# Feed-forward token tiles of 512, 512, 512 and 256 instead of four of 448, on one core

## The chip, the core and the metric

The program runs on one core of one Trainium2 chip. The metric is the device time of one execution in microseconds (us), the median of several runs. A core has a matrix engine (PE in the profile, with PEld for its weight loads), a vector engine (DVE), a scalar engine (ACT), a POOL engine that does next to nothing here, and SP, which issues the DMA transfers.

## What is computed

Three stages in a row: sigmoid attention over 4 batches x 12 heads x 448 tokens, then a feed-forward block with a maximum over three projections, then one with a slope for negative values. In short:

```
scores = scale * q @ k.T - log(S)                # 4 x 12 heads, S = 448, head_dim 64
x = sigmoid(scores) @ v                          # -> 1792 tokens x 768
h = max(max(x @ w1, x @ w2), x @ w3)             # 768 -> 768
y = h @ w_out                                    # 768 -> 768
p = y @ w_in                                     # 768 -> 2048
g = max(p, 0) + alpha * min(p, 0)
out = g @ w_out2                                 # 2048 -> 768
```

The weights come as 64-bit floats, viewed as pairs of 32-bit words; everything else is 32-bit.

## The kernel before

All activations lie with features on the 128 partitions and tokens along the free axis. For accuracy every feed-forward operand is split into a high and a low part, both of type float32r, and a product is made of three matmuls: weight-low x token-high, weight-high x token-low, weight-high x token-high. Weight loads and matmuls come in pairs: each matmul has a weight load of its own.

**Attention.** 24 pairs (batch b, pair of heads p). For each pair: 24 matmuls into `sc` (four chunks of keys, three products, two heads in the two halves of the rows), four sigmoids on ACT (L278), and 16 float32 matmuls of the pair before into `pav` (L287). ACT then copies `pav` into the high part `xh` (L297) and DVE subtracts to get the low part `xl` (L298).

**Feed-forward.** Tokens are cut into four tiles of 448, one for each batch. One accumulation in PSUM is a group: for a tile t and 128 output features, all inner blocks times three products. Stages are named by their PSUM tile: `b` (three projections, 18 weight units, 18 matmuls to a group), `c` (output of the first block, 6 units, 18 matmuls), then eight rounds of `d` (two units, 18 matmuls to a group) and `e` (6 groups for each t, each 6 matmuls over the two blocks of that round). All these matmuls are issued in `group` (L356). PSUM has 8 buffers for them (`ps_m`). DVE and ACT take the sums out: a copy or maximum for `b`, a split for `c`, the slope function for `d`, and for `e` an addition into `acc` (L488; in the first round a copy).

The work around the matmuls is in a hand-written order. `pending` holds the steps that turn a raw weight unit into its high and low part (8 per half unit, 6 of them on DVE); after each group of `b` and `c` 6 of them are issued (`run_pending(6)`), in `d` 8 and in `e` 2 per group (`weave`). In the last `e` round each finished `acc` is transposed on DVE one group later (`finish`, L420), and `store` (L504) sends it out in four transfers: a whole tile at a time, the last tile in two cuts.

Of the kernel before, what the change touches and what calls it, by code (L numbers as in the profile page):

```python
# [19 lines left out]
def kernel(  # L20
# [25 lines left out]

    nc = tc.nc

    B, H, S, D = q.shape
# [11 lines left out]
    HF = UN // 2  # L63
    scale = 1.0 / math.sqrt(D)
    neg_log_s = -math.log(S)

# [17 lines left out]
    SK = 2  # L84
# [108 lines left out]
            ops += [first, shift, sign, hi, power, rest, diff, lo]  # L193
        return ops

    def tmp(nm):
        return tpool.tile([P, S], F32, tag="tmp", name=nm, bufs=5)

    def xy_tile(nm, t):
        return (  # L200
            xpool.tile([P, KDM, S], F32R, tag=f"xyh{t}", name=f"{nm}h{t}"),
            xpool.tile([P, KDM, S], F32R, tag=f"xyl{t}", name=f"{nm}l{t}"),
        )


    def attention(apool, ps_s, ps_v):
# [73 lines left out]
        def av_pair(i):  # L280
            b, p = pairs[i]
            vt = prepped.pop(i)[-1]
            pav = ps_v.tile([P, 512], F32, tag="pv", name=f"pav{i}")
            for c in range(NCH):
                a = at.pop((i, c))
                for j in range(2):
                    nc.tensor.matmul(  # L287
                        pav[j * D : (j + 1) * D, :S],
                        vt[:, j * NCH + c, :],
                        a[:, j, :],  # L290
                        start=(c == 0),
                        stop=(c == NCH - 1),
                    )
            if p == 0:
                xt[b] = xy_tile("x", b)
            xh, xl = xt[b]
            nc.scalar.copy(xh[:, p, :], pav[:, :S])  # L297
            nc.vector.tensor_sub(xl[:, p, :], pav[:, :S], xh[:, p, :].bitcast(F32))  # L298

        n = len(pairs)  # L300
        load_pair(0)
# [31 lines left out]
    xt, yt, ht = {}, {}, {}  # L333


    def terms(n, wu, col, src):

        hi, lo = wu

        def cross(r):  # L340
            xh, xl = src(r)
            return [(lo[:, col(r)], xh), (hi[:, col(r)], xl)]

        def main(r):
            return [(hi[:, col(r)], src(r)[0])]

        got = []
        for r in range(n - 1):
            got += cross(r)
        for r in range(n - 1):  # L350
            got += main(r)
        return got + cross(n - 1) + main(n - 1)

    def group(ps, mms):
        for z, (lt, rh) in enumerate(mms):
            nc.tensor.matmul(ps, lt, rh, start=(z == 0), stop=(z == len(mms) - 1))  # L356

    def rowcol(r):
        return slice(r * P, (r + 1) * P)
# [4 lines left out]
        for _ in range(min(n, len(pending))):  # L364
            pending.pop(0)()

    def hl(pool, tag, nm):
        return (
            pool.tile([P, S], F32R, tag=f"{tag}h", name=f"{nm}h"),
            pool.tile([P, S], F32R, tag=f"{tag}l", name=f"{nm}l"),  # L370
        )

    def split(dst, src):
        hi, lo = dst
        nc.scalar.copy(hi, src)
        nc.vector.tensor_sub(lo, src, hi.bitcast(F32))

    def ff1(hpool, ps_m):
        u = 0
        for m in range(KF1):  # L380
            cur = {}
            for j in range(3):
                if u:
                    pending.extend(conv_ops(u + 1))
                for t in range(B):
                    ps = ps_m.tile([P, 512], F32, tag="mm", name=f"b{m}_{j}_{t}")[:, :S]
                    group(ps, terms(KDM, wsp[u], rowcol, lambda r: (xt[t][0][:, r, :], xt[t][1][:, r, :])))
                    run_pending(6)
                    if j == 0:
                        cur[t] = tmp(f"mx{m}_{t}")  # L390
                        nc.scalar.copy(cur[t], ps)
                    else:
                        nc.vector.tensor_tensor(out=cur[t], in0=ps, in1=cur[t], op=ALU.max)  # L393
                    if j == 2:
                        ht[m, t] = hl(hpool, f"h{m}_{t}", f"h{m}_{t}")
                        split(ht[m, t], cur[t])
                run_pending(99)
                wsp.pop(u)
                u += 1
        for m in range(KDM):  # L400
            pending.extend(conv_ops(u + 1))
            for t in range(B):
                ps = ps_m.tile([P, 512], F32, tag="mm", name=f"c{m}_{t}")[:, :S]
# [4 lines left out]
                yh, yl = yt[t]  # L408
                split((yh[:, m, :], yl[:, m, :]), ps)
            run_pending(99)  # L410
            wsp.pop(u)
            u += 1
        return u

    def ff2(gpool, ps_m, u):
# [2 lines left out]

        def finish(t, m, a, o):
            nc.vector.transpose(out=o[:, :, m, :], in_=a.rearrange("p (n i) -> p n i", i=32))  # L420
            cuts = [KDM] if t < B - 1 else [2, KDM]
            if m + 1 in cuts:
                store(t, ([0] + cuts)[cuts.index(m + 1)], m + 1, o)

        late, turn = [], []

        def prelu(m, t, ps, g):
            r_, n_ = tmp(f"r{m}_{t}"), tmp(f"n{m}_{t}")

            def parts():  # L430
                nc.scalar.activation(r_, ps, AF.Relu)
                nc.scalar.activation(n_, ps, AF.Relu, scale=-1.0)  # L432
# [12 lines left out]

            return [parts, join, hi, lo]
# [9 lines left out]
        for s in range(NS):  # L456
            pending.extend(conv_ops(u + SK))
            pending.extend(conv_ops(u + SK + 1))
            for f in range(SK):
                for t in range(B):  # L460
                    ps = ps_m.tile([P, 512], F32, tag="mm", name=f"d{s}_{f}_{t}")[:, :S]
                    group(ps, terms(KDM, wsp[u], rowcol, lambda r: (yt[t][0][:, r, :], yt[t][1][:, r, :])))
                    gt[f, t] = hl(gpool, f"g{f}_{t}", f"g{SK * s + f}_{t}")
# [7 lines left out]
            for t in range(B):  # L471
                if last:
                    ot[t] = xpool.tile([P, NB32, KDM, 32], F32, tag=f"xyh{t}", name=f"o{t}")
                for m in range(KDM):
                    ps = ps_m.tile([P, 512], F32, tag="mm", name=f"e{s}_{m}_{t}")[:, :S]
                    mms = []
                    for f in range(SK):
                        hi, lo = (x[:, m * P : (m + 1) * P] for x in wsp[u + f])
                        gh, gl = gt[f, t]
                        mms += [(lo, gh), (hi, gl), (hi, gh)]  # L480
                    group(ps, mms)
                    weave(late, 2)
                    late = []
                    if s == 0:
                        acc[m, t] = gpool.tile([P, S], F32, tag=f"acc{m}_{t}", name=f"acc{m}_{t}")
                        nc.scalar.copy(acc[m, t], ps)
# [12 lines left out]


    def store(t, m0, m1, o):
        for g in range(4):
            c0 = g * (DM // 4)
            nc.sync.dma_start(  # L504
                out=out[t * S : (t + 1) * S, c0 + 32 * m0 : c0 + 32 * m1].rearrange(
                    "(n i) f -> i n f", i=32
                ),
                in_=o[32 * g : 32 * g + 32, :, m0:m1, :].rearrange("i n m j -> i n (m j)"),
            )
# [53 lines left out]
```

## Time and profile before

| | |
|---|---|
| time, median of 3 runs | 984.21 us (983.95 to 984.31) |
| the profiled execution: time / span of its instructions | 984.14 us / 982.4 us |
| PE busy / DVE busy / ACT busy | 98% / 65% / 37% of the span |
| matmuls, and weight loads | 4992 of each |
| of these in the feed-forward stages (`b`, `c`, `d`, `e`) | 4032 |
| bytes read / written | 60.56 MB / 5.51 MB |

The span runs from the first to the last instruction; 1.7 us of the execution lie around it. A busy time is the union of the instructions of an engine; matmuls overlap one another, so the time that one adds is read from the distance between two starts and not from its own duration.

### The profile page before, as it was taken

The page shows a single profiled execution, that of the slowest core. Times are in us where ns is not written, and L with a number is a line of the kernel's source. Part 1 is how long each engine was busy: PE and PEld are TensorE (multiplying, and loading weights), DVE is VectorE, ACT ScalarE, POOL GpSimd, SP SyncE. Part 2 cuts the span into 40 slices and gives each one's busy share as a digit, 9 for nine tenths or more (in the row PEclk, how much of TensorE's full clock was granted, in tenths as well). Part 3 has the DMA queues.
Part 4 walks back from the last instruction along what each step waited for, and adds up shares of the span by engine and source line. Part 5 has one row for each costly group of instructions (what it writes and reads, how often), then busy time and mean ns, then how long its engine had stood idle before and what let it go on. Part 6 is the DMA issues. An engine that isn't in the chain of part 4 may idle for free.

```text
span 982.4 us, 12885 instructions
## 1 busy us (share of the span) xinstructions
PE 962.8 (98%) x4992; PEld 831.7 (85%) x4992; DVE 639.4 (65%) x1257; ACT 360.2 (37%) x635; POOL 0.2 (0%) x4
## 2 busy tenths in 40 slices
PE   6999999999999999999999999999999999999995
PEld 3455557999999999999999999999999999999994
DVE  5667771655464565565578368868587785869765
ACT  5677772122221222122236552332414334152410
POOL 0000000000000000000000000000000000000000
PEclk9999999999999999999999999999999999999998
DMA  7777750211221112112122122212122121212017
GB/s 128 134 148 139 136 106 1 65 49 49 65 65 47 51 49 63 51 51 62 50 67 76 51 65 64 65 33 57 41 65 65 49 66 33 65 49 65 17 39 186
DMA packets 158990, 66.92 MB, mean 68 GB/s; under 512 B 116944, under 2 KB 154832, under 8 KB 158928
## 3 DMA queue, kind: packets, MB, share of 16 engines
q1 hardware_dynamic: 158928, 66.09, 27.4%
q8 instruction: 39, 0.64, 0.3%
q14 instruction: 23, 0.19, 0.1%
HBM read 60.56 MB, written 5.51 MB: 67 GB/s over the span
## 4 chain that ended last, share of the span: by engine, by line
PE 98%; SPq 1%; DVE 0%; DMA 0%; issue 0%; DVEq 0%
PE b L356 27%; PE e L356 24%; PE d L356 24%; PE c L356 9%; PE pav L287 8%; PE sc L271 7%; SPq L222 1%; DMA kr<-in_k_dram 0%; DVE kt L243 0%; DVE qt L243 0%; DVE acc L488 0%; DVE o L420 0%; DVEq L559 0%; SPq L229 0%; DVE qh L250 0%
## 5 line engine op out<-in xcount | busy, mean ns | idle before, releaser
L174 ACT CAST wh<-wt 128x384 fp32r<-128x384 f32 x112 | 57.6, 514 | 290.8 <-DVE wt L161 290.8
L356 PE MATMUL b<-xh,wl 128*128 128x448 f32 x432 | 158.0, 366 | 0.0
L356 PE MATMUL b<-xl,wh 128*128 128x448 f32 x432 | 158.0, 366 | 0.0
L356 PE MATMUL d<-yl,wh 128*128 128x448 f32 x384 | 140.4, 366 | 0.0
L356 PE MATMUL d<-yh,wl 128*128 128x448 f32 x384 | 140.4, 366 | 0.0
L488 DVE TENSOR_TENSOR acc<-e,acc 128x448 f32<-128x448 f32 x168 | 102.8, 618 | 19.1 <-PE e L356 17.7
L356 PE MATMUL b<-xh,wh 128*128 128x448 f32 x432 | 111.0, 366 | 0.0
L356 PE MATMUL d<-yh,wh 128*128 128x448 f32 x384 | 98.7, 366 | 0.0
L278 ACT ACTIVATE a<-sc,bias_s 112x896 f32<-112x896 f32 x96 | 89.1, 1008 | 14.9 <-PE sc L271 14.5
L356 PEld LDWEIGHTS b<-xh,wl 128*128 128x128 f32 x432 | 81.2, 188 | 7.1 <-issue 0.7
L356 PEld LDWEIGHTS b<-xh,wh 128*128 128x128 f32 x432 | 81.2, 188 | 6.3
L356 PEld LDWEIGHTS b<-xl,wh 128*128 128x128 f32 x432 | 81.3, 188 | 6.2
L158 DVE TENSOR_SCALAR wt<-wt 128x384 uint32<-128x384 uint32 x112 | 39.6, 353 | 71.1 <-ACT wt L150 71.0
L287 PE MATMUL pav<-a,vt 112*64 112x448 f32 x384 | 77.2, 545 | 0.0
L435 DVE SCALAR_TENSOR_TENSOR r<-n,nalpha,r 128x448 f32<-128x448 f32 x64 | 43.7, 683 | 51.4 <-ACT n L432 51.4
L356 PEld LDWEIGHTS d<-yh,wh 128*128 128x128 f32 x384 | 72.2, 188 | 5.6
L356 PEld LDWEIGHTS d<-yl,wh 128*128 128x128 f32 x384 | 72.2, 188 | 5.6
L356 PEld LDWEIGHTS d<-yh,wl 128*128 128x128 f32 x384 | 72.2, 188 | 5.6
L191 DVE TENSOR_TENSOR wl<-wt,ws 128x384 fp32r<-128x384 f32 x112 | 62.5, 558 | 4.8 <-DVE wt L188 0.5
L177 DVE SCALAR_TENSOR_TENSOR ws<-wr,ws 128x384 f32<-128x384 uint32 x112 | 62.5, 558 | 3.8
L161 DVE SCALAR_TENSOR_TENSOR wt<-wr,wt 128x384 uint32<-128x384 uint32 x112 | 62.3, 556 | 3.0
L393 DVE TENSOR_TENSOR mx<-b,mx 128x448 f32<-128x448 f32 x48 | 29.9, 623 | 52.1 <-PE b L356 52.1
(97 smaller groups left out, 1566.4 us busy)
## 6 DMA issues: line engine op xcount, KB each, us to landing
wr<-in_moe_w_out_dram SPq DMA_DIRECT2D x44, 384.0 KB, 3.1
wr<-in_moe_w_dram SPq DMA_DIRECT2D x36, 384.0 KB, 3.2
wr<-in_moe_w_in_dram SPq DMA_DIRECT2D x32, 384.0 KB, 3.2
kr<-in_k_dram SPq DMA_DIRECT2D x96, 56.0 KB, 3.3
qr<-in_q_dram SPq DMA_DIRECT2D x96, 56.0 KB, 2.6
vt<-in_v_dram SPq DMA_DIRECT2D x24, 224.0 KB, 3.5
out_dram<-o SPq DMA_DIRECT2D x12, 336.0 KB, 5.4
out_dram<-o SPq DMA_DIRECT2D x4, 224.0 KB, 3.9
```

The source lines that it names most:

```text
L158: nc.vector.tensor_scalar(st["T"], st["T"], 3, None, ALU.logical_shift_left)
L161: nc.vector.scalar_tensor_tensor(out=st["T"], in0=st["r"][:, :, 1], scalar=0x80000000, in1=st["T"], op0=ALU.bitwise_and, op1=ALU.bitwise_or,)
L174: nc.scalar.copy(part(0), seen(st["T"]))
L177: nc.vector.scalar_tensor_tensor(out=st["R"].bitcast(F32), in0=st["r"][:, :, 0], scalar=2.0**-52, in1=st["R"].bitcast(F32), op0=ALU.mult, ...
L191: nc.vector.tensor_add(part(1), seen(st["T"]), seen(st["R"]))
L271: nc.tensor.matmul(sc[:KC, j, :S], kk[r, c * KC : (c + 1) * KC], qq[r], start=(z == 0), stop=(z == 2),)
L278: nc.scalar.activation(a, sc[:KC, :, :S], AF.Sigmoid, bias=bias_s[:KC], scale=scale)
L287: nc.tensor.matmul(pav[j * D : (j + 1) * D, :S], vt[:, j * NCH + c, :], a[:, j, :], start=(c == 0), stop=(c == NCH - 1),)
L356: nc.tensor.matmul(ps, lt, rh, start=(z == 0), stop=(z == len(mms) - 1))
L393: nc.vector.tensor_tensor(out=cur[t], in0=ps, in1=cur[t], op=ALU.max)
L435: nc.vector.scalar_tensor_tensor(out=r_, in0=n_, scalar=nalpha[:, m : m + 1], in1=r_, op0=ALU.mult, op1=ALU.add,)
L488: nc.vector.tensor_tensor(out=acc[m, t], in0=ps, in1=acc[m, t], op=ALU.add)
```

## The change

The 1792 tokens are cut without regard to the batches: three tiles of 512 and one of 256. In the last tile the high and the low part of the tokens lie side by side in one 512-wide tile, so that weight-high is multiplied with both in one matmul of 512 columns; weight-low takes the high part alone, 256 columns. The sum then stands in two halves of a PSUM tile, which `whole` adds up (an ACT copy of one half and a DVE addition) before it is used; in `e` both halves are added into `acc` one after the other. The attention copies a batch's columns into the one or two token tiles that they fall in.

```diff
+    T = B * S
+    TW = 512
+    spans = [(c, min(TW, T - c)) for c in range(0, T, TW)]
+    NT = len(spans)
+    HW = spans[-1][1]
...
+            parts = []
+            for t, (c0, w) in enumerate(spans):
+                c, e = max(c0, b * S), min(c0 + w, b * S + S)
+                if c < e:
...
+            for xh, _, ps in parts:
+                nc.scalar.copy(xh, ps)
+            for xh, xl, ps in parts:
+                nc.vector.tensor_sub(xl, ps, xh.bitcast(F32))
...
         def cross(r):
-            xh, xl = src(r)
+            xh, xl, both = src(r)
+            if both is not None:
+                return [(hi[:, col(r)], both), (lo[:, col(r)], xh)]
             return [(lo[:, col(r)], xh), (hi[:, col(r)], xl)]
...
+    def whole(ps, t, nm):
+
+        if t < NT - 1:
+            return ps
+        s = tmp(nm, t)
+        nc.scalar.copy(s, ps[:, HW:])
+        nc.vector.tensor_tensor(out=s, in0=ps[:, :HW], in1=s, op=ALU.add)
+        return s
...
-                    else:
-                        nc.vector.tensor_tensor(out=acc[m, t], in0=ps, in1=acc[m, t], op=ALU.add)
+                        nc.scalar.copy(acc[m, t], ps[:, TW - w :])
+                    for h in range(s == 0, TW // w):
+                        part = ps[:, TW - (h + 1) * w : TW - h * w]
+                        nc.vector.tensor_tensor(out=acc[m, t], in0=part, in1=acc[m, t], op=ALU.add)
```

On PE, in the last `e` round, the first group of the last token tile (`e_0_3`: feature block 0, tile 3; `g_3` are the tokens, `wh` and `wl` the weights) before the change:

```order
L356 MATMUL e_0_3_8671<-g_3h,wl_8250 128x448
L356 MATMUL e_0_3_8671<-g_3l,wh_8249 128x448
L356 MATMUL e_0_3_8671<-g_3h,wh_8249 128x448
L356 MATMUL e_0_3_8671<-g_3h,wl_8325 128x448
L356 MATMUL e_0_3_8671<-g_3l,wh_8324 128x448
L356 MATMUL e_0_3_8671<-g_3h,wh_8324 128x448
```

The same place now, with the last two matmuls of the 512-wide tile ahead of it:

```order
L382 MATMUL e_5_2_8499<-g_2l,wh_8170 128x512
L382 MATMUL e_5_2_8499<-g_2h,wh_8170 128x512
L382 MATMUL e_0_3_8509<-g_3_8202,wh_8095 128x512
L382 MATMUL e_0_3_8509<-g_3_8202,wl_8096 128x256
L382 MATMUL e_0_3_8509<-g_3_8320,wh_8170 128x512
L382 MATMUL e_0_3_8509<-g_3_8320,wl_8171 128x256
```

The group has four matmuls, of 512 and 256 columns in turn; the groups of the other three tiles keep their number and are 512 wide.

On DVE, in the same round, before: one addition into `acc` for each group, and behind it the transposition of the group before.

```order
L488 TENSOR_TENSOR acc_2_5052<-e_5_2_8661,acc_2_5052 128x448
L420 STREAM_TRANSPOSE o_8611<-acc_2_5043 128x14x32
L488 TENSOR_TENSOR acc_3_5061<-e_0_3_8671,acc_3_5061 128x448
L420 STREAM_TRANSPOSE o_8611<-acc_2_5052 128x14x32
L488 TENSOR_TENSOR acc_3_5070<-e_1_3_8684,acc_3_5070 128x448
L420 STREAM_TRANSPOSE o_8670<-acc_3_5061 128x14x32
```

And now:

```order
L534 TENSOR_TENSOR acc_2_4988<-e_5_2_8499,acc_2_4988 128x512
L460 STREAM_TRANSPOSE o_8449<-acc_2_4979 128x16x32
L534 TENSOR_TENSOR acc_3_4995<-e_0_3_8509,acc_3_4995 128x256
L534 TENSOR_TENSOR acc_3_4995<-e_0_3_8509,acc_3_4995 128x256
L460 STREAM_TRANSPOSE o_8449<-acc_2_4988 128x16x32
L534 TENSOR_TENSOR acc_3_5003<-e_1_3_8521,acc_3_5003 128x256
L534 TENSOR_TENSOR acc_3_5003<-e_1_3_8521,acc_3_5003 128x256
L460 STREAM_TRANSPOSE o_8508<-acc_3_4995 128x8x32
```

In the last tile two additions stand for one, the second reading what the first wrote; the transpositions keep their places.

On ACT in the attention, at the first pair of the second batch, before: the copy of `pav` stands between the last sigmoid of one pair and the first of the next.

```order
L278 ACTIVATE a_2_644<-sc_2_643,bias_s 112x896
L278 ACTIVATE a_3_655<-sc_3_654,bias_s 112x896
L297 CAST xh_676<-pav_667 128x448
L278 ACTIVATE a_0_700<-sc_0_699,bias_s 112x896
L278 ACTIVATE a_1_711<-sc_1_710,bias_s 112x896
```

And now:

```order
L291 ACTIVATE a_2_644<-sc_2_643,bias_s 112x896
L291 ACTIVATE a_3_655<-sc_3_654,bias_s 112x896
L316 CAST xh_248<-pav_667 128x64
L316 CAST xh_676<-pav_667 128x384
L291 ACTIVATE a_0_702<-sc_0_701,bias_s 112x896
L291 ACTIVATE a_1_713<-sc_1_712,bias_s 112x896
```

Two copies stand where one stood, in the 18 pairs of the second to the fourth batch (64 and 384, 128 and 320, 192 and 256 columns); the subtractions on DVE are doubled in the same way.

## Rows read from the trace of the kernel before

**Rows 1.** The page, engines: busy time, share of span, instructions.
```profile
PE 962.8 (98%) x4992; PEld 831.7 (85%) x4992; DVE 639.4 (65%) x1257; ACT 360.2 (37%) x635; POOL 0.2 (0%) x4
```

**Rows 2.** The chain that ended last, in time: start us, us, what.
```profile
153.71 262.86 PE b L356 x1296
416.56 87.55 PE c L356 x432
504.11 29.19 PE d L356 x144
...
941.87 29.20 PE e L356 x144
971.10 0.62 DVE acc L488
971.72 0.55 DVE o L420
```

**Rows 3.** Busy time by stretch, a round of d and e: granted clock after engines.
```profile
820.00:920.00 100.00, 100.00 (x495) 92.78 (x494) 77.54 (x155) 31.07 (x63) 0.00 (x0) 1.00 0.18 52
```

**Rows 4.** Timeline, weight loads and matmuls where the feed-forward begins: start, us.
```profile
153.64 0.19 PEld L356 LDWEIGHTS b<-xh,wl 128*128 128x128 f32 x1 [0.70 <-issue]
153.75 0.19 PEld L356 LDWEIGHTS b<-xl,wh 128*128 128x128 f32 x1
153.95 0.19 PEld L356 LDWEIGHTS b<-xh,wl 128*128 128x128 f32 x1
...
153.95 0.37 PE L356 MATMUL b<-xl,wh 128*128 128x448 f32 x1
```

**Rows 5.** Weight loads by shape: count, busy us, mean ns of one.
```profile
L356 PEld LDWEIGHTS b<-xl,wh 128*128 128x128 f32 x432 | 81.3, 188 | 6.2
L271 PEld LDWEIGHTS sc<-ql,kh 64*112 64x112 f32 x192 | 17.2, 176 | 3.4 <-DVE ql L251 0.5
```

**Rows 6.** Timeline of PE in attention, matmuls into sc.
```profile
19.50 0.36 PE L271 MATMUL sc<-qh,kl 64*112 64x448 f32 x2
...
20.31 0.37 PE L271 MATMUL sc<-ql,kh 64*112 64x448 f32 x2
```

**Rows 7.** Timeline of weight loads for pav, first and last of six.
```profile
16.47 0.14 PEld L287 LDWEIGHTS pav<-a,vt 112*64 112x64 f32 x2 [0.23 <-issue]
...
18.34 0.14 PEld L287 LDWEIGHTS pav<-a,vt 112*64 112x64 f32 x2 [0.23 <-issue]
```

**Rows 8.** Timeline in the attention, between two pairs, PE, ACT and DVE.
```profile
35.19 0.63 DVE L251 TENSOR_TENSOR ql<-qt,qh 128x448 fp32r<-128x448 f32 x1
37.14 0.46 PE L271 MATMUL sc<-qh,kh 64*112 64x448 f32 x2
37.26 0.53 ACT L297 CAST xh<-pav 128x448 fp32r<-128x448 f32 x1 [1.42 <-PE pav L287]
38.10 2.80 ACT L278 ACTIVATE a<-sc,bias_s 112x896 f32<-112x896 f32 x3 [0.31 <-PE sc L271]
```

**Rows 9.** Groups of ACT and DVE by shape: count, busy us, mean ns.
```profile
L331 ACT ACTIVATE nalpha<-alpha_sb 128x16 f32<-128x16 f32 x1 | 0.2, 218 | 0.0
L488 DVE TENSOR_TENSOR acc<-e,acc 128x448 f32<-128x448 f32 x168 | 102.8, 618 | 19.1 <-PE e L356 17.7
L420 DVE STREAM_TRANSPOSE o<-acc 128x448 f32<-128x448 f32 x24 | 15.0, 630 | 0.0
```

**Rows 10.** Timeline in b: a unit's last conversion, the next unit's first matmul.
```profile
193.74 0.56 DVE L191 TENSOR_TENSOR wl<-wt,ws 128x384 fp32r<-128x384 f32 x1
...
197.52 0.36 PE L356 MATMUL b<-xh,wl 128*128 128x448 f32 x1
```

**Rows 11.** The stores: their queue's timeline, their sizes, the stretch's DMA share and GB/s.
```profile
952.13 26.23 SPq L504 DMA_DIRECT2D out_dram<-o  x20
...
out_dram<-o SPq DMA_DIRECT2D x12, 336.0 KB, 5.4
...
952.00:981.00 29.00, 19.06 (x95) 17.33 (x93) 20.26 (x36) 0.00 (x0) 0.00 (x0) 0.90 0.80 191
```

More of the change, by code (lines that the diff above doesn't have):

```diff
@@ L194, in conv_ops, with tmp, three @@
         return ops
-    def tmp(nm):
-        return tpool.tile([P, S], F32, tag="tmp", name=nm, bufs=5)
+    def tmp(nm, t):
+        return tpool.tile([P, TW], F32, tag="tmp", name=nm, bufs=5)[:, : spans[t][1]]
+    def three(x):
+        return x[:, 0], x[:, 1], x.rearrange("p a n -> p (a n)")
     def xy_tile(nm, t):
[L200 to L203, printed above, removed]
+        if t == NT - 1:
+            x = xpool.tile([P, KDM, 2, HW], F32R, tag=f"xyh{t}", name=f"{nm}{t}")
+            return [three(x[:, r]) for r in range(KDM)]
+        h = xpool.tile([P, KDM, TW], F32R, tag=f"xyh{t}", name=f"{nm}h{t}")
+        l = xpool.tile([P, KDM, TW], F32R, tag=f"xyl{t}", name=f"{nm}l{t}")
+        return [(h[:, r], l[:, r], None) for r in range(KDM)]
     def attention(apool, ps_s, ps_v):
@@ L293, in av_pair @@
                     )
[L294 to L298, printed above, removed]
+            parts = []
+            for t, (c0, w) in enumerate(spans):
+                c, e = max(c0, b * S), min(c0 + w, b * S + S)
+                if c < e:
+                    if t not in xt:
+                        xt[t] = xy_tile("x", t)
+                    xh, xl, _ = xt[t][p]
+                    parts.append((xh[:, c - c0 : e - c0], xl[:, c - c0 : e - c0], pav[:, c - b * S : e - b * S]))
+            for xh, _, ps in parts:
+                nc.scalar.copy(xh, ps)
+            for xh, xl, ps in parts:
+                nc.vector.tensor_sub(xl, ps, xh.bitcast(F32))
         n = len(pairs)
@@ L340, in cross @@
         def cross(r):
-            xh, xl = src(r)
+            xh, xl, both = src(r)
+            if both is not None:
+                return [(hi[:, col(r)], both), (lo[:, col(r)], xh)]
             return [(lo[:, col(r)], xh), (hi[:, col(r)], xl)]
         def main(r):
-            return [(hi[:, col(r)], src(r)[0])]
+            xh, xl, both = src(r)
+            return [] if both is not None else [(hi[:, col(r)], xh)]
         got = []
@@ L355, in group @@
         for z, (lt, rh) in enumerate(mms):
-            nc.tensor.matmul(ps, lt, rh, start=(z == 0), stop=(z == len(mms) - 1))
+            w = rh.shape[-1]
+            nc.tensor.matmul(ps[:, :w], lt, rh, start=(z == 0), stop=(z == len(mms) - 1))
+    def whole(ps, t, nm):
[5 more added lines that the diff above has]
+        return s
     def rowcol(r):
@@ L365, in run_pending, with hl @@
             pending.pop(0)()
-    def hl(pool, tag, nm):
+    def hl(pool, tag, nm, t):
+        if t == NT - 1:
+            return three(pool.tile([P, 2, HW], F32R, tag=f"{tag}h", name=nm))
         return (
-            pool.tile([P, S], F32R, tag=f"{tag}h", name=f"{nm}h"),
-            pool.tile([P, S], F32R, tag=f"{tag}l", name=f"{nm}l"),
+            pool.tile([P, TW], F32R, tag=f"{tag}h", name=f"{nm}h"),
+            pool.tile([P, TW], F32R, tag=f"{tag}l", name=f"{nm}l"),
+            None,
         )
     def split(dst, src):
-        hi, lo = dst
+        hi, lo, _ = dst
         nc.scalar.copy(hi, src)
@@ L384, in ff1 @@
                     pending.extend(conv_ops(u + 1))
-                for t in range(B):
-                    ps = ps_m.tile([P, 512], F32, tag="mm", name=f"b{m}_{j}_{t}")[:, :S]
-                    group(ps, terms(KDM, wsp[u], rowcol, lambda r: (xt[t][0][:, r, :], xt[t][1][:, r, :])))
+                for t in range(NT):
+                    ps = ps_m.tile([P, TW], F32, tag="mm", name=f"b{m}_{j}_{t}")
+                    group(ps, terms(KDM, wsp[u], rowcol, lambda r: xt[t][r]))
                     run_pending(6)
-                    if j == 0:
-                        cur[t] = tmp(f"mx{m}_{t}")
+                    if j == 0 and t < NT - 1:
+                        cur[t] = tmp(f"mx{m}_{t}", t)
                         nc.scalar.copy(cur[t], ps)
-                    else:
-                        nc.vector.tensor_tensor(out=cur[t], in0=ps, in1=cur[t], op=ALU.max)
+                    elif j == 0:
+                        cur[t] = whole(ps, t, f"mx{m}_{t}")
+                    else:
+                        got = whole(ps, t, f"b{m}_{j}s")
+                        nc.vector.tensor_tensor(out=cur[t], in0=got, in1=cur[t], op=ALU.max)
                     if j == 2:
-                        ht[m, t] = hl(hpool, f"h{m}_{t}", f"h{m}_{t}")
+                        ht[m, t] = hl(hpool, f"h{m}_{t}", f"h{m}_{t}", t)
                         split(ht[m, t], cur[t])
@@ L401, in ff1 @@
             pending.extend(conv_ops(u + 1))
-            for t in range(B):
-                ps = ps_m.tile([P, 512], F32, tag="mm", name=f"c{m}_{t}")[:, :S]
+            for t in range(NT):
+                ps = ps_m.tile([P, TW], F32, tag="mm", name=f"c{m}_{t}")
                 group(ps, terms(KF1, wsp[u], rowcol, lambda r: ht[r, t]))
@@ L407, in ff1 @@
                     yt[t] = xy_tile("y", t)
-                yh, yl = yt[t]
-                split((yh[:, m, :], yl[:, m, :]), ps)
+                split(yt[t][m], whole(ps, t, f"c{m}s"))
             run_pending(99)
@@ L427, in prelu @@
         def prelu(m, t, ps, g):
[L428 removed]
+            r_, n_ = tmp(f"r{m}_{t}", t), tmp(f"n{m}_{t}", t)
             def parts():
[L431 to L432 removed]
+                s = whole(ps, t, f"s{m}_{t}")
+                nc.scalar.activation(r_, s, AF.Relu)
+                nc.scalar.activation(n_, s, AF.Relu, scale=-1.0)
             def join():
@@ L459, in ff2 @@
             for f in range(SK):
[L460 to L463, printed above, removed]
+                for t in range(NT):
+                    ps = ps_m.tile([P, TW], F32, tag="mm", name=f"d{s}_{f}_{t}")
+                    group(ps, terms(KDM, wsp[u], rowcol, lambda r: yt[t][r]))
+                    gt[f, t] = hl(gpool, f"g{f}_{t}", f"g{SK * s + f}_{t}", t)
                     weave(late, 8 if s else 10)
@@ L470, in ff2 @@
                 pending.extend(conv_ops(u + SK + f))
-            for t in range(B):
+            for t in range(NT):
+                w = spans[t][1]
                 if last:
-                    ot[t] = xpool.tile([P, NB32, KDM, 32], F32, tag=f"xyh{t}", name=f"o{t}")
+                    ot[t] = xpool.tile([P, w // 32, KDM, 32], F32, tag=f"xyh{t}", name=f"o{t}")
                 for m in range(KDM):
-                    ps = ps_m.tile([P, 512], F32, tag="mm", name=f"e{s}_{m}_{t}")[:, :S]
+                    ps = ps_m.tile([P, TW], F32, tag="mm", name=f"e{s}_{m}_{t}")
                     mms = []
@@ L478, in ff2 @@
                         hi, lo = (x[:, m * P : (m + 1) * P] for x in wsp[u + f])
-                        gh, gl = gt[f, t]
-                        mms += [(lo, gh), (hi, gl), (hi, gh)]
+                        gh, gl, both = gt[f, t]
+                        if both is not None:
+                            mms += [(hi, both), (lo, gh)]
+                        else:
+                            mms += [(lo, gh), (hi, gl), (hi, gh)]
                     group(ps, mms)
@@ L501, in store @@
     def store(t, m0, m1, o):
+        r0, w = spans[t]
         for g in range(4):
@@ L504, in store @@
             nc.sync.dma_start(
-                out=out[t * S : (t + 1) * S, c0 + 32 * m0 : c0 + 32 * m1].rearrange(
+                out=out[r0 : r0 + w, c0 + 32 * m0 : c0 + 32 * m1].rearrange(
                     "(n i) f -> i n f", i=32
```

6 lines of the change are left out of this document (3 added, 3 removed).

## The prediction

> **What bounds the kernel now.** The page comes first: PE is busy for 98% of the span, DVE for 65%, ACT for 37% [rows 1]. The chain that ended last shows where that binds: from 153.71 to 971.1 us it is PE alone, stage after stage, with nothing between them [rows 2]. The matmuls of `b`, 1296, take 262.86 us, those of `c`, 432, take 87.55, and a `d` or `e` of 144 takes 29.2 [rows 2]: 262.86/1296 = 202.8 ns and 87.55/432 = 202.7 ns from one matmul to the next. So the time of the feed-forward is 4032 matmuls times a pitch of 202.7 ns, 817 us, and a change is worth what it does to that product unless another engine begins to hold PE up. After PE comes a tail of about 11 us in which DVE adds and transposes and the stores run out.
>
> **The matmuls.** For each weight block (128 x 128, high and low) there were 4 x 3 = 12 matmuls of 448 columns. There are now 9 of 512, one of 512 for both parts of the short tile, and one of 256: 11, with 5376 columns as before. 4032/12 = 336 blocks. Write the pitch as a + b x columns: twelve times 448 and the new eleven differ by exactly a, once per block. The whole gain is therefore the part of the 202.7 ns that does not grow with the columns, and no row shows it directly, since every matmul before is 448 wide.
>
> Bounds for a from rows. Below: if the pitch grows in proportion, a = 0. Above: the columns cannot be free, and the nearest row for their price is `pav`, also 448 columns of 32-bit tokens: six pairs of loads start between 16.47 and 18.34 us [rows 7], so a pair of matmuls takes 1.87/5 = 374 ns, 187 ns for each 448 columns. That leaves a = 202.7 - 187 = 15.7 ns and b = 187/448 = 0.417 ns. The granted clock is 1.00, the 2.4 GHz level [rows 3], so this is no throttled stretch. I take 15.7: `pav` shows that 448 columns of 4-byte tokens can go in faster than the feed-forward takes them, which a plain limit on the read rate does not explain. Against it: `pav` is of another type (float32, two matmuls side by side), and its 187 may be a different mode.
>
> Is the pitch set by the weight load instead? A load is shown as 188 ns [rows 5] and starts with the matmul before it; 188 is near 202.7. Two rows speak against it. In the attention the loads have 112 columns and take 176 ns [rows 5], but `sc` pairs start at 19.50 and, four pairs on, at 20.31 [rows 6]: 0.81/4 = 202.5 ns, the same pitch with a shorter load. And where the feed-forward begins, with no matmul in flight, the second load starts 0.11 us after the first (153.64, 153.75), and its matmul only at 153.95 [rows 4]: a load occupies its path for about 110 ns, the rest of the 188 is latency.
>
> The Trainium skill (TensorE: Matmul & The Clock Gate, section LDWEIGHTS) gives a load columns/1.2 GHz, 107 ns for 128 columns; the first distance agrees. The same page (Back-to-back issue gap) gives N/2.4 + 2.5 ns between matmuls, 189.2 for 448; this trace has 202.7, so the measurement decides. If its 2.5 ns were all that is constant, the gain would be 0.8 us and the change would not be seen.
>
> So a 512-wide matmul costs 202.7 + 64 x 0.417 = 229.4 ns, and a 256-wide one 202.7 - 192 x 0.417 = 122.6. For the latter the range is wide: 115.8 in proportion, 202.7 if the load's whole duration stands behind it. I take 122.6, just above the 110 ns of a load that hides under the matmul before. Block: 10 x 229.4 + 122.6 = 2416.6 against 12 x 202.7 = 2432.4, 15.7 ns less. The last `e` has 144/12 = 12 blocks, the stages ahead of it 324: 324 x 15.7 = 5.1 us earlier.
>
> **Who could hold PE up.** *Attention.* 18 pairs get a second ACT copy. After the copy of `pav` ACT idles 0.31 us until the first `sc` is done [rows 8]. The smallest ACT operation in the trace takes 218 ns [rows 9]; a split copies the same 448 columns, so at most that is added, and 0.31 covers it: nothing. If each piece cost a full 0.53, 0.22 x 18 = 4.0 us would reach PE. DVE's second subtraction delays the next pair's preparation; its last step ends at 35.82 and is needed at 37.14 [rows 8], 1.3 us of cover against at most 0.22 + 0.63.
>
> *Weights in `b`.* The last conversion of a unit ends at 194.30, the next unit's first matmul is at 197.52 [rows 10]: 3.2 us. Its steps stand behind the maximum of the second tile, which comes 2 x 18 x 26.7 ns = 0.96 us later; some 2 us stay.
>
> *Extra DVE and ACT work.* `whole` runs 40 times (18 + 6 + 16 groups), `e` has 48 more additions counting the first round's. At 618 ns for 448 columns [rows 9], 256 lie between 353 (in proportion) and 618; with 0.4 us DVE gains 88 x 0.4 = 35 us on 639, and in a round of `d` and `e` some 3 us in 58, on 77% busy [rows 3]. With 8 PSUM buffers behind it nothing reaches PE; if the cover were gone, each `e` would lose what two additions (0.8 us) exceed a short group (704 ns) by, 0.1 x 6 x 8 = 5 us.
>
> *The tail.* 5.51 MB go out from 952.13 on, 191 GB/s on average until 981 [rows 11]: the stores run back to back and the end is their start plus 29 us. The first tile's store starts 952.13 - 941.87 = 10.26 us into the last `e`. Its 36 groups' worth of matmuls now take 36 x 229.4 = 8.26 instead of 7.30 us, so it may start up to 1.0 us later; before, DVE was behind at that point and can use some of it. I take 0.7 us (0 to 1.1). In the short tile DVE needs two additions and a transposition for each 704 ns of PE, between 6 x 1.07 and 6 x 1.87 us (in proportion and at the full 618 and 630 ns [rows 9]): it ends 3 to 8 us after PE. That only hides because the queue of stores is longer still.
>
> **Sum.** The profiled execution took 984.14 us, 0.07 under the median: 984.14 - 5.1 + 0.7 = **979.8 us**, 0.45% less.
>
> **Rivals.** A measurement of this kernel tells about 0.2%, 2 us, from no change: faster is below 982.2, slower above 986.2.
>
> *The pitch grows with the columns* (a near 0, or given back by the copies in the attention). For it: no row shows two widths, and `sc` and the feed-forward have one pitch at one width. Against it: `pav`. Matmuls save nothing, the tail costs 0.7: 984.8.
>
> *The short matmul waits for its next load.* The side that ends slower. After each 256-wide matmul PE needs the high weights of the next block, and only the short matmul hides that load. If the load shows at its full 188 ns plus the 14.7 up to the next matmul, the 256 columns cost 202.7, not 122.6: 80.1 x 324 = 26 us, 1005.8. It decides from 122.6 + 4.4/0.324 = 136 ns on; above 142 ns the kernel is slower. For it: the load starts only when the matmul before it starts. Against it: the 110 ns of rows 4.
>
> *The load sets the pitch already*, at 202.7 for any width up to it. Then 512 columns cost 512 x 0.417 = 213.7 and 256 cost 202.7: 2339.7 per block, 92.7 less, 984.1 - 30 + 0.7 = 955. The equal pitch of `sc` speaks against it.
>
> **How the numbers follow.** My forecast (a of 10 to 16, short matmul under 130 ns) 52%; growth in proportion 22%; the short matmul waits 22%, of which 4 between 982.2 and 986.2; the load sets it already 4%. Faster 52 + 4 = 56%, same 22 + 4 = 26%, slower 18%. The forecast alone spans 978.5 to 981.5; with the second case and the near end of the third, 978 to 988 holds 80%.
>
> **What the profile after would show.** 3696 feed-forward matmuls; in the chain `b` at 1188 matmuls and 261.2 us (108 x 15.7 ns less), `c` 87.0, `d` and `e` 29.0 each, PE still alone. Starts 229 ns apart in the 512-wide groups; in the short ones 229 and 123 in turn. If the full groups show 231.6 and the short 116, the pitch is in proportion; if the gap behind a 256-wide matmul is near 200, the load is exposed. The tail from PE's end to the span's end should grow from 11.3 us to about 12. An idle PE before `sc` longer than before, or before the first matmul of a unit, would show a cover that failed, and make the prediction wrong.

## The result, and the profile after

| | before | after | forecast |
|---|---|---|---|
| time, median | 984.21 us | 973.74 us (973.55 to 974.06) | 979.8 (978 to 988) |
| ratio | | 0.9894, 95% interval 0.9877 to 0.9911 | 0.9955 |
| the profiled execution: time / span | 984.14 / 982.4 | 973.74 / 971.6 | |

The change gained 10.5 us, more than twice the forecast. The page of the kernel after, engines (busy time, share of the span, instructions):

```profile
PE 950.1 (98%) x4656; PEld 744.2 (77%) x4656; DVE 677.4 (70%) x1363; ACT 373.5 (38%) x687; POOL 0.2 (0%) x4
```

As forecast there are 336 matmuls fewer, and DVE has 38 us more to do. The chain that ended last, against [rows 2] (start us, us, what):

```profile
153.99 258.70 PE b L382 x1188
412.69 86.16 PE c L382 x396
498.85 28.72 PE d L382 x132
...
929.65 24.50 PE e L382 x108
954.15 0.02 issue
954.17 0.69 DVE acc L534
...
962.12 0.35 DVE o L460
```

PE is still alone up to the last tile of the last `e`; only its last 24 matmuls now end before the additions that the chain follows. A block costs 258.70/108 = 2395 ns in `b` and 28.72/12 = 2393 in `d` and `e`, against 262.86/108 = 2434 and 29.19/12 = 2432: 39 ns less, where 15.7 were forecast. The last `e` starts at 929.65 instead of 941.87, 12.2 us earlier (forecast 5.1), and from there to the span's end it takes 41.95 instead of 40.5 us, 1.4 longer (forecast 0.7).

The timeline of PE where the first short group begins (start us, us):

```profile
165.84 0.39 PE L382 MATMUL b<-xl,wh 128*128 128x512 f32 x1
166.07 0.39 PE L382 MATMUL b<-xh,wh 128*128 128x512 f32 x1
166.29 0.39 PE L382 MATMUL b<-x,wh 128*128 128x512 f32 x1
166.52 0.28 PE L382 MATMUL b<-x,wl 128*128 128x256 f32 x1
166.63 0.40 PE L382 MATMUL b<-x,wh 128*128 128x512 f32 x1
166.87 0.28 PE L382 MATMUL b<-x,wl 128*128 128x256 f32 x1
```

Starts among 512-wide matmuls of the full tiles lie 226.9 ns apart (mean of 3024 distances, nearly all of them 226 or 227; forecast 229.4). In the short tile 235.0 and 117.0 in turn (means of 336 and 335), 352.0 for the two, which is what the forecast's 229.4 + 122.6 add up to. So the pair was right in sum, and the 512-wide matmul alone 2.5 ns too dear: 9 x 2.5 = 22.5 ns per block, the difference between 15.7 and 38.3 (12 x 202.7 less 9 x 226.9 and 352.0). A line through 448 and 512 has 24.2 ns for 64 columns, 0.378 ns each, less than one cycle of the 2.4 GHz level. That makes it doubtful that the price by width is one line, and the experiments begin there.

### The profile page after: what moved, and what is told of

Its sections match the earlier page's. It is cut to its first block, busy times and chain, and to the rows that moved or that the text cites. A ratio compares the mean times of both kernels' runs of the same rounds, so it can differ in the third digit from the quotient of the medians.

```text
span 971.6 us, 12420 instructions
## 1 busy us (share of the span) xinstructions
PE 950.1 (98%) x4656; PEld 744.2 (77%) x4656; DVE 677.4 (70%) x1363; ACT 373.5 (38%) x687; POOL 0.2 (0%) x4
## 4 chain that ended last, share of the span: by engine, by line
PE 97%; DVE 1%; SPq 1%; DMA 0%; issue 0%; DVEq 0%
PE b L382 27%; PE d L382 24%; PE e L382 23%; PE c L382 9%; PE pav L300 8%; PE sc L284 7%; SPq L235 1%; DVE acc L534 1%; DMA kr<-in_k_dram 0%; DVE o L460 0%; DVE kt L256 0%; DVE qt L256 0%; SPq L242 0%; DVE qh L263 0%; DVE kh L263 0%
## 5 line engine op out<-in xcount | busy, mean ns | idle before, releaser
L534 DVE TENSOR_TENSOR acc<-e,acc 128x512 f32<-128x512 f32 (+1 forms) x216 | 120.6, 573 | 9.8 <-ACT acc L531 6.6
L382 PE MATMUL b<-xh,wl 128*128 128x512 f32 x324 | 126.3, 390 | 0.0
L382 PE MATMUL b<-xl,wh 128*128 128x512 f32 x324 | 126.1, 389 | 0.0
L382 PE MATMUL d<-yh,wl 128*128 128x512 f32 x288 | 112.2, 390 | 0.0
L382 PE MATMUL d<-yl,wh 128*128 128x512 f32 x288 | 112.0, 389 | 0.0
L291 ACT ACTIVATE a<-sc,bias_s 112x896 f32<-112x896 f32 x96 | 89.2, 1010 | 13.9 <-PE sc L284 13.5
L382 PE MATMUL b<-xh,wh 128*128 128x512 f32 x324 | 91.0, 389 | 0.0
L382 PE MATMUL d<-yh,wh 128*128 128x512 f32 x288 | 80.9, 389 | 0.0
L476 DVE SCALAR_TENSOR_TENSOR r<-n,nalpha,r 128x512 f32<-128x512 f32 x64 | 43.8, 685 | 44.5 <-ACT n L473 44.4
L382 PEld LDWEIGHTS d<-yh,wl 128*128 128x128 f32 x288 | 54.1, 188 | 11.5
L157 ACT ACTIVATE wt<-wr 128x384 f32<-128x384 f32 x112 | 61.8, 552 | 0.0
L195 DVE TENSOR_TENSOR wt<-wt,wh 128x384 f32<-128x384 f32 x112 | 61.7, 551 | 0.0
```

What stands on the lines that cost most here:

```text
L157: nc.scalar.activation(st["T"].bitcast(F32), st["r"][:, :, 1].bitcast(F32), AF.Abs, scale=2.0**-112,)
L195: nc.vector.tensor_sub(seen(st["T"]), seen(st["T"]), part(0).bitcast(F32))
L291: nc.scalar.activation(a, sc[:KC, :, :S], AF.Sigmoid, bias=bias_s[:KC], scale=scale)
L382: nc.tensor.matmul(ps[:, :w], lt, rh, start=(z == 0), stop=(z == len(mms) - 1))
L476: nc.vector.scalar_tensor_tensor(out=r_, in0=n_, scalar=nalpha[:, m : m + 1], in1=r_, op0=ALU.mult, op1=ALU.add,)
L534: nc.vector.tensor_tensor(out=acc[m, t], in0=part, in1=acc[m, t], op=ALU.add)
```

## The experiments

Three things were open: whether the gain belongs to fewer matmuls or to their width, what a matmul costs by its width, and what sets the tail. Times are medians; before was 984.2 us beside each.

### What a matmul costs by width

Series of 60 matmuls in one small kernel, each with its own weight load, in float32r unless named:

```diff
+        section("n512", 60, f(512))
...
+        section("n448", 60, f(448))
+        section("p448", 60, f(448, x448))
...
+        section("n256", 60, f(256))
...
+        section("n128", 60, f(128))
+        section("a512x256", 60, alt(512, 256))
...
+        section("bf448", 60, lambda k: (wbf[k % NX], xb[:, k % NX, :448]))
...
```

> This kernel leaves out the whole computation: it issues 21 series of 60 matmuls on one core (each matmul with a weight load of its own, six to an accumulation, widths 512 down to 128, some from tiles of another stride, some alternating, some with 64 weight columns, some in bfloat16) and stores a constant. It measures the distance of starts by width. The three distances known so far are 202.7 ns at 448, 226.7 at 512, and 352.0 for a 512 and a 256 together. Line theory (a constant plus a price per column through the two known points, 34.7 + 0.375 x columns): 214.7 at 480, 178.7 at 384, 154.7 at 320, 130.7 at 256. Step theory (the column price of pav, 0.417, plus 13.3 ns always, plus some 2.7 more at every width but 512): 216.0 at 480, 176.0 at 384, 149.3 at 320, 122.7 at 256. Stride theory (the 2.7 come from rows of 448 elements that lie 1792 bytes apart): 448 columns out of a 512-wide tile take 200.0, out of a 448-wide tile 202.7. Load theory (the load sets a floor): below some width the distance stops falling, near 110 ns or near 190, and with 64 weight columns it falls further. If the constant belongs to the type float32r, bfloat16 shows less than 13 ns over its columns.

The granted clock is 1.00 in every stretch from 30 us on (the 2.4 GHz level); a first series, which runs ahead of that, is not counted. The busy time by stretch (the clock stands behind the engines), and on the timeline of PE the two series of 448 columns, out of a tile of 448 and out of one of 512 with an offset, and the next:

```profile
30.00:93.00 63.00, 63.00 (x296) 55.33 (x295) 0.67 (x4) 0.00 (x0) 0.00 (x0) 1.00 0.00 1
93.00:180.00 87.00, 87.00 (x544) 82.97 (x543) 1.50 (x9) 0.00 (x0) 0.00 (x0) 1.00 0.00 1
```

```profile
81.30 12.32 PE L88 MATMUL p<-x,wt 128*128 128x448 f32 x60
93.46 12.32 PE L88 MATMUL o<-x,wt 128*128 128x448 f32 x60
105.62 51.13 PE L88 MATMUL n<-x,wt 128*128 128x416 f32 x360
```

From one series to the next it is 12.16 us for 60 matmuls in both, 202.7 ns: the stride theory falls. A second kernel filled in more widths:

```diff
+        for nn in (504, 488, 472, 464, 456, 448, 440, 432, 424, 400, 352, 288, 240):
+            section(f"n{nn}", 60, f(nn))
+        section("psame", 60, pair_same)
+        section("pkern", 60, pair_kernel)
+        section("pwide", 60, pair_wide)
+        section("pruns", 60, runs, 12)
...
```

> This kernel leaves out the whole computation, like the first series: 20 series of 60 matmuls. Widths in float32r: if the extra over columns/2.4 + 13.3 ns belongs to widths between 416 and 496 alone, 504 and 400, 352, 288 show 13.3 and 488 to 424 show up to 17; if it belongs to certain multiples, it comes and goes between them. 240 columns: the load's floor of 111.7 or columns + 13.3 = 113.3. Pairs of 512 and 256: with the same tokens for both matmuls, with weights out of a 768-wide tile, with both as in the kernel, and six of each in a row; whichever shows 352 for a pair where the first series had 346.7 names the cause of the kernel's 5.3 ns.

Mean distance of starts (50 of each series), and what it exceeds columns/2.4 by:

| columns | ns | over columns/2.4 | | columns | ns | over columns/2.4 |
|---|---|---|---|---|---|---|
| 512 | 226.7 | 13.3 | | 432 | 195.9 | 15.9 |
| 504 | 226.7 | 16.7 | | 416 | 186.7 | 13.3 |
| 496 | 220.0 | 13.3 | | 400 | 180.0 | 13.3 |
| 480 | 216.7 | 16.7 | | 384 | 173.5 | 13.5 |
| 464 | 208.9 | 15.6 | | 320 | 146.7 | 13.3 |
| 456 | 208.7 | 18.7 | | 256 | 120.0 | 13.3 |
| 448 | 202.7 | 16.0 | | 240 | 112.0 | 12.0 |
| 440 | 200.0 | 16.7 | | 224 and 128 | 111.7 | floor |
| 352 | 161.2 | 14.5 | | 288 | 131.7 | 11.7 |
| 488 | 220.0 | 16.7 | | 472 | 213.3 | 16.7 |
| 424 | 193.3 | 16.7 | | 512, 64 weight columns | 230.1 | 16.8 |
| 448, 64 weight columns | 202.2 | 15.5 | | 256, 64 weight columns | 113.3 | 6.7 |
| bfloat16, 448 | 189.2 | 2.5 | | bfloat16, 256 | 109.2 | 2.5 |

Three things follow. From 256 to 512 columns a float32r matmul with 128 weight columns costs 106.7 ns more, 0.417 for each column, one cycle of the 2.4 GHz level; beside its columns it pays 13.3 ns at either width, bfloat16 2.5. The widths from 424 to 504 that were tried pay 2 to 5 ns more, except 496; 448 is one of them (352 and 288 stand a little off on either side). Of these, 504, 488, 472, 440 and 424 cost what the next multiple of 16 would cost at 13.3; but 480, 464, 448 and 432, multiples themselves, lie 2 to 3 ns above theirs, and no run shows why. And the distances stop falling at 111.7 ns, not at 188 or 202.7.

That the weight load sets this floor is argued and not shown: it is near the 0.11 us between two loads of [rows 4], but no run changed the load at a narrow width. With 64 weight columns the distance is nearly unchanged at 448 (202.2), so the load does not set the pace there; at 256 it is shorter (113.3 instead of 120.0), so the 13.3 ns depend on the load in part; and at 512 it is longer (230.1), which stays open.

The line theory (130.7 at 256) falls; the step theory holds with its second step at certain widths alone. The Trainium skill (TensorE: Matmul & The Clock Gate, Back-to-back issue gap) gives N/2.4 + 2.5 ns for a matmul whose load is not counted: the bfloat16 series agree, though each of their matmuls has a load, and the float32r ones at 512 and 256 are 10.8 ns above it. The Trainium skill (same page, section LDWEIGHTS) gives 107 ns for a load of 128 columns, 5 ns under the floor.

A 512 and a 256 in turn took 346.7 ns in the first kernel, the sum of 226.7 and 120.0; a 512 and a 448 in turn took 437.8 there, 8.4 more than their sum. In the second kernel three variants took 353.3 (10.60 us for 30 pairs), with the same tokens for both (`psame`), with weights out of a wide tile (`pwide`), or with both as in the feed-forward (`pkern`); six of each in a row (`pruns`) took some 350 for a pair. Their starts on the timeline:

```profile
176.74 10.76 PE L88 MATMUL psame<-x,wt 128*128 128x512 f32 x60
187.34 10.76 PE L88 MATMUL pkern<-x,ww 128*128 128x512 f32 x60
197.94 10.76 PE L88 MATMUL pwide<-x,ww 128*128 128x512 f32 x60
208.53 10.64 PE L88 MATMUL pruns<-x,ww 128*128 128x512 f32 x60
219.02 25.95 PE L88 MATMUL w<-x,ww 128*128 128x448 f32 x120
```

The same shapes have more than one price, and the cause is open: the sequence of the first kernel was not run again in the second, and each variant differs from it in the tokens, in the weights or in both. Weights out of a wide tile cost nothing by themselves: in the last two series (`w`) they give 202.7 at 448 and 226.7 at 512, as before.

### The tile widths without the one pass

The short tile makes three matmuls of 256 columns per block, 12 in all as before:

```diff
-        return x[:, 0], x[:, 1], x.rearrange("p a n -> p (a n)")
+        return x[:, 0], x[:, 1], None
...
```

> The changed kernel, but the short tile makes three matmuls of 256 columns for each block (and no halves to add), so a block has 12 matmuls as before: it has the tile widths of the change without the one pass over both parts. Line theory: 9 x 226.7 + 3 x 130.7 = 2432, no gain over the kernel before apart from the tail, about 985 us. Step theory: 9 x 226.7 + 3 x 122.7 = 2408, 24 ns less than before and 16 more than the change: 324 x 16 = 5.2 us over the changed kernel, about 979 us. Theory of the prediction (one constant of 15.7 per matmul): the gain all goes, about 984.8 us.

975.93 us, ratio 0.9916 (0.9899 to 0.9932). Its chain:

```profile
153.98 259.76 PE b L382 x1296
413.75 86.52 PE c L382 x432
500.26 28.84 PE d L382 x144
...
932.73 24.52 PE e L382 x108
```

As many matmuls as before, and yet the last `e` starts 9.1 us earlier than before [rows 2]. A block costs 28.84/12 = 2403 ns, 29 less (its 512-wide distances average 227.1, its 256-wide 119.6); the one pass of the change takes off another 10. So some three quarters of the gain is the widths' and a quarter the missing matmul's. The forecast of one constant per matmul (984.8) falls; the step theory had the size of the block right (2408) and the time 3 us too high: the one pass is worth 10 ns per block instead of 16, and the tail is 0.5 us shorter (974.1 - 932.7 = 41.4), as the first store starts 10.9 us into the last `e` (943.65) instead of 11.5.

### Other widths

Tiles of 384, 384, 512 and 512, three matmuls each, as a second test of the widths with 12 matmuls:

```diff
-    spans = [(c, min(TW, T - c)) for c in range(0, T, TW)]
+    spans = [(0, 384), (384, 384), (768, 512), (1280, 512)]
...
```

> Token tiles of 384, 384, 512 and 512, three matmuls each: 12 matmuls to a block as before, no pass over both parts, nothing to add up. Width theory (the gain came mostly from leaving the width 448, which pays 16.0 ns over its columns where 384 and 512 pay 13.3 in the series): a block takes 6 x 226.7 + 6 x 173.4 = 2400 ns against 2432 of the kernel before, 32 x 324 = 10.4 us less in the path, 973 to 975 us with a tail like the one before or 1 us longer. One constant per matmul (the prediction): as many matmuls, no gain, 984 us.

978.4 us, ratio 0.9937 (0.9919 to 0.9954): a miss of 3 us on the width theory, though far from no gain. Its chain:

```profile
154.01 260.58 PE b L382 x1296
414.59 86.80 PE c L382 x432
501.39 28.93 PE d L382 x144
...
934.92 28.88 PE e L382 x144
```

The last `e` starts 7.0 us earlier than before, where 10.4 was expected: a block costs 28.93/12 = 2411 ns, since the 512-wide distances average 227.7 here and the 384-wide 174.0, up to 1 ns above the series. And the tail from there on takes 976.8 - 934.9 = 41.9 us, as long as that of the change. Its first store starts early, 9.4 us into the last `e` (944.33), but then the stores move little for a while (DMA share and GB/s last; more on this under the tail):

```profile
956.00:960.00 4.00, 4.00 (x20) 3.30 (x18) 3.85 (x7) 0.00 (x0) 0.00 (x0) 1.00 0.30 73
```

What the change of widths adds to the distances in the real stream was not followed further.

### The order in the short group

The 512-wide matmuls of all but the last inner block of a group first, then their 256-wide ones, then the last block's two (in `e`, both blocks' 512-wide ones first). That leaves 128 of the 336 changes from 512 to 256 columns:

```diff
-                return [(hi[:, col(r)], both), (lo[:, col(r)], xh)]
+                return [(hi[:, col(r)], both)]
...
-            return [] if both is not None else [(hi[:, col(r)], xh)]
+            return [(lo[:, col(r)], xh)] if both is not None else [(hi[:, col(r)], xh)]
...
```

> The changed kernel with another order inside a group of the short tile: the 512-wide matmuls of several blocks one after the other, then the 256-wide ones, instead of 512 and 256 in turn. In the changed kernel a 512 and a 256 in turn take 352.0 ns; the series gave 226.7 for 512 alone, 120.0 for 256 alone and 346.7 for the two in turn. If the 5.3 ns come from the turn-taking, most of 336 x 5.3 = 1.8 us goes: about 972.0 us. If they come from something else in the kernel (the weights' place, the tokens), nothing changes: 973.7 us.

974.02 us, ratio 0.9895 (0.9877 to 0.9912): no change. The 256-wide ones are 117.3 ns apart, but distances among the 512-wide ones rise from 226.9 to 227.6 on average, and `b` takes 259.01 us instead of 258.70. The 5.3 ns per pair move elsewhere and are not gone; their cause stays open.

### The tail

First the first tile alone in two cuts:

```diff
-            cuts = [KDM] if t < NT - 1 else [2, KDM]
+            cuts = [3, KDM] if t == 0 else [KDM] if t < NT - 1 else [2, KDM]
```

> The changed kernel, but in the last round the first tile is stored in two cuts (three feature blocks, then three) instead of one. If the end is set by stores that run back to back from the first one on, the first starts three groups, 4.1 us, earlier and the time falls by 3 to 4 us, to about 970 us. If the end is set by the last tile (its additions, its two cuts and the wait for earlier transfers), it falls by less than 1 us.

973.69 us, no change. The stores begin 3.4 us earlier than in the change (941.19) and then stop; first the timeline of the queue that issues them, then by stretch, behind the clock, the DMA share and GB/s:

```profile
937.79 31.01 SPq L551 DMA_DIRECT2D out_dram<-o  x24
```

```profile
942.00:946.00 4.00, 4.00 (x20) 3.30 (x19) 4.00 (x7) 0.00 (x0) 0.00 (x0) 1.00 0.92 198
946.00:950.00 4.00, 4.00 (x19) 3.34 (x18) 3.85 (x7) 0.00 (x0) 0.00 (x0) 1.00 0.17 38
950.00:954.00 4.00, 4.00 (x20) 3.30 (x19) 3.85 (x7) 0.00 (x0) 0.00 (x0) 1.00 0.84 181
```

So an earlier first store alone does not move the end: the stores stand still while the second tile is being made. In the change itself they did not, and there they run back to back, as the prediction had it:

```profile
946.00:950.00 4.00, 4.00 (x19) 3.30 (x19) 3.89 (x6) 0.00 (x0) 0.00 (x0) 1.00 0.86 203
...
958.00:962.00 4.00, 0.36 (x3) 0.03 (x1) 3.86 (x11) 0.00 (x0) 0.00 (x0) 0.94 0.83 180
```

Then all three tiles in two cuts:

```diff
-            cuts = [KDM] if t < NT - 1 else [2, KDM]
+            cuts = [3, KDM] if t < NT - 1 else [2, KDM]
```

> The changed kernel with all three 512-wide tiles stored in two cuts in the last round. Run before this one: two cuts of the first tile alone started the stores 4.1 us earlier and moved the end by nothing, with an idle transfer queue between the first tile's and the second's. If the end is set by the whole store of the third tile, which can only start when its last feature block is transposed, half of its bytes now leave 4 us earlier and the time falls by 2 to 4 us, to 970 to 972 us. If the end is set by the last tile's own cuts, it falls by less than 1 us.

969.86 us, ratio 0.9853 (0.9836 to 0.987), 3.9 us under the change. The chain where the last `e` starts, the stretch in which the run before this one stood still, and the timeline of the queue:

```profile
929.80 24.50 PE e L382 x108
```

```profile
946.00:950.00 4.00, 4.00 (x19) 3.34 (x18) 3.85 (x7) 0.00 (x0) 0.00 (x0) 1.00 0.92 228
```

```profile
937.77 27.26 SPq L551 DMA_DIRECT2D out_dram<-o  x32
```

The same queue in the change, where it issues 20 transfers:

```profile
941.19 27.38 SPq L551 DMA_DIRECT2D out_dram<-o  x20
```

It begins 3.4 us earlier and is done 3.5 us earlier (965.0 against 968.6), and from the start of the last `e` to the span's end it is now 968.0 - 929.80 = 38.2 us instead of 41.95. From the first store to the span's end it takes 30.2 us, as in the kernel before (982.4 - 952.1) and nearly as in the change (30.4); with the first tile alone in two cuts it took 34.0. So the runs fit an end that lies some 30 us behind the first store where the later tiles follow without a gap. Which of the later cuts closed the gap was not separated. The same edit on the kernel before:

```diff
-            cuts = [KDM] if t < B - 1 else [2, KDM]
+            cuts = [3, KDM] if t < B - 1 else [2, KDM]
```

> The kernel before, with its first three tiles stored in two cuts in the last round. If the stores' gain of 3.9 us in the changed kernel is the end of a tail that both kernels have, this falls by 2 to 4 us, to 980 to 982 us. If whole tiles of 448 leave in time and only those of 512 are late, it stays within 1 us of 984.2.

981.62 us, ratio 0.9973 (0.9961 to 0.9984): 2.6 us less, as expected: the gain of the halves is no matter of the 512-wide tiles alone, though it is 1.3 smaller than theirs. The first store starts 3.0 us earlier (949.16), and from there to the span's end it takes 30.9 us. Then thirds, for the last tile too:

```diff
-            cuts = [KDM] if t < NT - 1 else [2, KDM]
+            cuts = [2, 4, KDM]
```

> The changed kernel with every tile, the last too, stored in three cuts of two feature blocks. Halves gave 969.9 us. If what is left of the tail is bytes that wait for their cut, it falls by another 0.5 to 1.5 us; if it is the cost of issuing more and smaller transfers one after the other, it rises by up to 2 us.

971.38 us, ratio 0.9867 (0.9851 to 0.9882), 1.5 above the halves. Its queue, and the last stretches (DMA share and GB/s last):

```profile
936.36 30.64 SPq L551 DMA_DIRECT2D out_dram<-o  x48
```

```profile
962.00:966.00 4.00, 0.00 (x0) 0.00 (x0) 0.72 (x3) 0.00 (x0) 0.00 (x0) 0.53 0.60 138
966.00:969.00 3.00, 0.00 (x0) 0.00 (x0) 0.00 (x0) 0.00 (x0) 0.00 (x0) 0.50 0.37 87
```

48 transfers keep the queue issuing until 967.0, 2 us longer than the 32 of the halves, and meanwhile the stores move only 138 and 87 GB/s, where those of the halves moved 174 from 962 to 966. The queue issues almost without a pause from 936.36 on, which speaks for the cost of issuing; from the first store to the span's end it takes 33.0 us. Last, the grouped order and the halves together, the edits shown for both:

```diff
-                            mms += [(hi, both), (lo, gh)]
+                            mms.insert(f, (hi, both))
+                            mms.append((lo, gh))
...
-            cuts = [KDM] if t < NT - 1 else [2, KDM]
+            cuts = [3, KDM] if t < NT - 1 else [2, KDM]
```

> The two edits before this one together: the sum of what they give alone, 968.5 to 971.5 us if both work, 973.7 us if neither does.

970.41 us, ratio 0.9857 (0.9837 to 0.9876): the grouping adds nothing to the halves. In this profile the feed-forward began only at 155.65, 1.7 us later than after the change, so the comparison is not finer than that. The halves alone are the fastest version of all, 3.9 us under the change.

## Why the prediction was wrong, point by point

- **PE bounds the kernel from 153.7 us to the tail**: right, before and after. No wait of PE came up in the feed-forward; weights and PSUM buffers were in time.
- **"Write the pitch as a + b x columns: twelve times 448 and the new eleven differ by exactly a"**: this step failed. It took the 202.7 ns at one width, with the column price of `pav`, for a point on a line that holds at every width, though it said itself that every matmul before is 448 wide. The series show 13.3 ns beside the columns at 512 and 256, and 2.7 more at 448. The change leaves 448 for all nine full matmuls: each takes 226.9 instead of the 229.4 of the line, 9 x 2.5 = 22.5 ns per block beside the 15.7. The kernel with 12 matmuls of 512 and 256 columns shows the gain without the missing matmul: 29 ns less per block; the missing one adds 10. The forecast could not see this, since a gain that comes with no fewer matmuls was not among its cases, save for the rival in which the load sets the pace. Why 448 costs more than 512 beside its columns is open.
- **a = 15.7 from `pav`**: as the constant at 448 it was right (16.0); as what one matmul less is worth it was too high (13.3 in the series, 10 in the kernel). Growth in proportion to the columns fell: it asked for 231.6 at 512 and 115.8 at 256, and the series have 226.7 and 120.0.
- **A 512-wide matmul at 229.4**: 226.9. **The pair with the short one at 352.0**: 352.0, partly by luck, since the series of the two alone add up to 346.7, and the parts were 235.0 and 117.0 instead of 229.4 and 122.6.
- **The weight load hides under 256 columns**: right. Distances down to 111.7 ns stand in the series, with a load for each matmul. The argument for it was weaker than it read: the matmul of the first load is shown from 153.64 on, so a matmul was in flight. The rival that should have ended slower, a load shown at 202.7, fell, and so did the load as pace-setter at 448.
- **The attention at nothing**: the feed-forward begins at 153.99 instead of 153.71; in the other changed kernels it was 153.67 to 154.16 (and once 155.65), so no loss that can be told apart. The smallest ACT operation before takes 204 ns and not 218; two copies took 0.70 us (213 and 486 ns for 64 and 384 columns) where one took 0.53, and the 0.31 us of cover is more than that.
- **35 us more on DVE, hidden**: 38, hidden from PE, but not in the tail.
- **The tail 0.7 us longer, because the first store starts later and all run back to back**: 1.4, and from PE's end 13.3 us (958.4 to 971.6) where about 12 were forecast. The reason holds and the size was wrong: the first store starts 11.5 us into the last `e` instead of 10.3, 1.3 later, and from there to the span's end it takes 30.4 us instead of 30.2. The term was worked out from the time that PE takes for the first tile, but DVE, which is still behind there, sets it. DVE at its first addition and at its sixth transposition of that round, before:

```profile
945.12 1.15 DVE L488 TENSOR_TENSOR acc<-e,acc 128x448 f32<-128x448 f32 x2
...
951.48 0.62 DVE L420 STREAM_TRANSPOSE o<-acc 128x448 f32<-128x448 f32 x1
```

And after:

```profile
933.31 1.28 DVE L534 TENSOR_TENSOR acc<-e,acc 128x512 f32<-128x512 f32 x2
...
940.47 0.69 DVE L460 STREAM_TRANSPOSE o<-acc 128x512 f32<-128x512 f32 x1
```

It gets there 3.66 us into the last `e` instead of 3.25, and the stretch from the one to the other takes 7.16 us instead of 6.36. What the prediction's sum leaves out, that the later tiles have to follow without a gap, does not bind in the change, but it does as soon as the first store is moved alone.

In sum: 12.2 us gained up to the last `e` instead of 5.1, 1.4 lost behind it instead of 0.7. Of the 10.8 us that this leaves, the time shows 10.5, since 2.1 us of the execution lie around the span now, where 1.7 did.

## What to carry to other kernels

Where every matmul in a profile has one width, its pitch says nothing of another width: measure a short series at the widths in question, in the type in question, before costing a change of tiles. In float32r take a width that pays only the constant in the series (512, 496, 416, 400, 384, 320, 256 here), and count the missing matmuls after that; in the whole kernel the distances came out up to 1 ns above the series. When tiles grow, look at when the first bytes can leave and whether the rest can follow without a gap: larger tiles stored whole start later, and two cuts of each gave back more than was lost.

## What the runs showed of the hardware

- float32r matmuls with a load of 128 weight columns each: 13.3 ns over columns/2.4 at 512, 496, 416, 400, 320 and 256 columns, between 15.6 and 18.7 at the widths tried from 424 to 504 other than 496; bfloat16 2.5 at 448 and 256. Neither the stride nor the start of the tokens matters at 448 (202.7 each).
- With 64 weight columns: 230.1 ns at 512, 202.2 at 448, 113.3 at 256.
- The least distance of two float32r matmuls with a load of 128 weight columns: 111.7 ns at 224 and at 128 columns, though the load is shown as 188.
- 512 and 256 columns in turn took 346.7 ns in one kernel, 353.3 in another with other tokens or weights, and 352.0 in the feed-forward. Why is open.
- 5.5 MB of stores out of one queue: 30.2 to 30.9 us from the first to the span's end with 20 or 32 transfers and no standstill, 33.0 with 48.
